# A gated linear attention with a SwiGLU layer behind it: every queue's order written out as a list

## The chip, the cores and the metric

The kernel runs on one core of a Trainium2 chip. The metric is the device time of one execution in microseconds; of the kernel before there are three runs. The core has five instruction queues that run at their own pace and wait for each other by semaphores: PE (TensorE, matmuls), DVE (VectorE), ACT (ScalarE), POOL (GpSimd) and SP (SyncE, which here only issues DMAs). Each queue works strictly in its order, so an instruction that waits holds all that stand behind it.

## The reference

For 4 sequences, 8 heads, 768 steps and a head size of 48, a state is rotated and shrunk by a complex gate at each step:

```python
mag = np.sqrt(a_re * a_re + a_im * a_im)
scale = np.minimum(mag, 0.999) / (mag + 1e-06)
for t in range(S):
    S_re, S_im = ar * S_re - ai * S_im + kv, ar * S_im + ai * S_re
    y[:, :, t] = np.einsum('bhd,bhde->bhe', q[:, :, t], S_re)
```

Here ar and ai are the scaled gate of the step, and kv is the outer product of k and v. The result, 3072 tokens by 384, is normalised by its root mean square and multiplied by a gain (rms_g), and goes through `silu(x @ w_gate) * (x @ w_val) @ w_out` with 1536 hidden columns. All of it is fp32. The weights reach the kernel as pairs of 32-bit words.

## The kernel before, in words

The sequence is cut into 24 chunks of 128 steps, numbered from 0. For each chunk, or each pair from chunk 2 on, `gates` (a generator) turns the gate into phase and magnitude. ACT makes squares, inverse roots, an arc tangent and sines; DVE makes running products and sums (scans), and multiplies q and k by cosine and sine into the tiles `rot` and `kin`. Six DMAs on SP then move these rows into `kq`; the text calls them the moves. A load of gate tables on ACT (`ACT_TABLE_LOAD`) stands wherever the function wanted is not in the tables that are active.

`attend` does one chunk. PE makes the scores of `kq` in small 32-row matmuls, DVE copies them under a causal mask into `am`, and PE multiplies by v (`ve`) and by the carried state. Another set of matmuls (`vn`, `kt`) and two DVE steps with the chunk's `decay` make the next state. For the norm, ACT squares, PE sums over features with a column of ones, DVE writes the mean to `ssv`, POOL raises it to the power -0.5 (`rs`), and for chunks 4 to 21 two DMAs on POOL spread that column to a row in every partition (`sq`, then `row`). DVE multiplies the chunk by `row` and so writes `xT`. For other chunks a matmul with the identity spreads it.

`feed`, `joint` and `down` do the feed-forward layer for two chunks, or for four at the end. `feed` multiplies directly for the first two pairs; `joint` does the later ones with fewer products and sums of weights and inputs on DVE and ACT; `down` is the down projection, whose results leave through `mid` and the two tiles `ot`, each sent by a DMA. The four banks that `feed`, `joint` and `down` share in PSUM are free again when the DVE additions into `ot` have read them. `narrow` makes fp32 weights out of the pairs of words, piece by piece: POOL issues the load, ACT one pass, DVE three passes, into `wg`, `wv` and `wo`. `look` loads the words again later, to test whether the narrowing was exact.

None of these functions issues anything. They call `add`, which notes an operation with its engine, its calls, an estimated duration, and the operations that it depends on (`box` and `note` find these from the slices read and written). When all 2976 are there, the planner (`Flow.schedule`) plays the engines through with these estimates, due times, margins for transfers and a table of shifts by stage (`flow.shift`), and at each step gives the engine the operation that is due first. `issue` then emits the operations in that order; every instruction carries the line of its loop, L751 before. `flow.warm` names one matmul as a filler. The planner puts fillers in front of a PE operation where it expects PE to be idle up to 62 us; they read `rot`, so they begin when the first `rot` row set is written.

A second path, `general`, for inputs that the fast one can't take, stands behind a flag that the fast path writes last (`bad`); it is not run here.

Of the kernel before, what the change touches and what calls it, by code (L numbers as in the profile page):

```python
# [18 lines left out]
P = 128  # L19
# [480 lines left out]

class Flow:
# [14 lines left out]
    MARGIN = {"load": 2.0, "kq": 2.0, "look": 2.0, "raw": 1.5, "attend": 1.5, "rot": 0.6, "decay": 0.6, "norm": 0.3}  # L516
    turn = 0.3
# [3 lines left out]
    TABLES = {"silu": ("S",), "sin": ("S", "N"), "arctan": ("T",), "rsqrt": ("A",)}  # L521

    def __init__(self, nc, rooms):
        self.nc = nc
        self.rooms = rooms
        self.ops = []
        self.seen = {}
        self.stage = None
        self.shift = {}
        self.warm = None  # L530
        self.fillers = []
# [19 lines left out]
    def box(self, ap):  # L551
        t = ap.tensor
        if t.name not in self.rooms:
            return None
        name, row = self.rooms[t.name]
        size = mybir.dt.size(ap.dtype)
        start = ap.offset * size
        p0, lo = divmod(start, row)
        np_, hi = 1, lo + size
        for step, n in ap.ap:  # L560
            if step * size > row:
                p0, np_ = p0 * n, n
            elif step * size == row:
                np_ += (n - 1) * (step * size // row)
            else:
                hi += (n - 1) * step * size
        return name, p0, p0 + np_, lo, hi

    def note(self, op, ap, write):
# [3 lines left out]
        name, p0, p1, lo, hi = b  # L573
        if name.startswith("bank"):
            p0, p1, lo, hi = 0, P, 0, 2048
        kept = []
        for x in self.seen.get(name, ()):
            o, w, q0, q1, l, h = x
            over = q0 < p1 and p0 < q1 and l < hi and lo < h
            if over and (write or w) and o != op["i"] and (not op["group"] or self.ops[o]["group"] != op["group"]):  # L580
                op["deps"].add(o)
            if op["group"] or not (write and p0 <= q0 and q1 <= p1 and lo <= l and h <= hi):
                kept.append(x)
        kept.append((op["i"], write, p0, p1, lo, hi))
# [19 lines left out]
    def dates(self):  # L604
        users = [[] for _ in self.ops]
        self.next = [[] for _ in self.ops]
        for op in self.ops:
            op["behind"] -= op["deps"]
            for d in op["deps"]:
                users[d].append(op["i"])  # L610
            for d in op["behind"]:
                self.next[d].append(op["i"])
        for op in reversed(self.ops):
            due = op["base"] if op["base"] is not None else 1e6
            for u in users[op["i"]]:
                x = self.ops[u]
                stretch = 1.0 if x["eng"] == "PE" else 1.35
                due = min(due, x["due"] - x["dur"] * stretch - (x["land"] or 0.0) - 0.2)
            op["due"] = due
        for op in self.ops:  # L620
            op["due"] += self.shift.get(op["stage"], 0.0)
            if op["late"] is not None:
                op["due"] = max(op["due"], op["late"])
        return users

    def schedule(self):
        users = self.dates()
        left = [len(op["deps"]) + len(op["behind"]) for op in self.ops]
        ready = [0.0] * len(self.ops)
        free = {eng: self.BEGIN.get(eng, 0.0) for eng in self.ENGINES}  # L630
        waiting = {eng: [] for eng in self.ENGINES}
        table = None
        mode = last = None
        for op in self.ops:
            if not left[op["i"]]:
                waiting[op["eng"]].append(op)
        queue = []
        sent = []
        recent = []
        served = held = quiet = 0.0  # L640
        order = 0

        def release(o, end, users=users):
            for u in users[o["i"]]:
                x = self.ops[u]
                margin = o["margin"] if users is not self.next and x["land"] is None and end > self.FROM else 0.0
                ready[u] = max(ready[u], end + self.delay(o, x) + margin)
                left[u] -= 1
                if not left[u]:
                    waiting[x["eng"]].append(x)  # L650

        def able(o):
            return max(ready[o["i"]], quiet) if o["grip"] else ready[o["i"]]

        while True:
            best = None
            for eng in self.ENGINES:
                ops = waiting[eng]
                if ops:
                    if eng == "POOL":  # L660
                        t = min(max(free[eng], ready[o["i"]], held + 0.01 if o["shy"] else 0.0) for o in ops)
                    else:
                        t = max(free[eng], min(able(o) for o in ops))
                    if eng == "SP" and len(sent) >= self.LANES:
                        if "landed" not in sent[-self.LANES]:
                            continue
                        t = max(t, sent[-self.LANES]["landed"])
                    if best is None or t < best[0]:
                        best = (t, eng)
            if queue:  # L670
                o = min(queue, key=lambda o: o["arrives"])
                t = max(served, o["arrives"])
                if best is None or t <= best[0]:
                    queue.remove(o)
                    served = t + o["load"] + 0.05
                    o["landed"] = served + o["slow"] + self.LAND
                    release(o, o["landed"])
                    continue
            if best is None:
                break  # L680
            t, eng = best
            pick = None
            for o in waiting[eng]:
                if able(o) > t + 1e-9 or o["shy"] and t < held:
                    continue
                key = o["due"]
                if o["table"] and table not in self.TABLES[o["table"]]:
                    key += self.switch if t > self.FROM else 4.0
                if eng == "PE" and o["mode"] != mode and t > self.FROM:
                    key += self.turn  # L690
                if pick is None or key < pick[0]:
                    pick = (key, o)
            o = pick[1]
            if eng in self.patient:
                if any(t < able(x) < t + o["dur"] - 0.2 and x["due"] < o["due"] - 50.0 and able(x) < t + 1.5 for x in waiting[eng]):
                    free[eng] = max(free[eng], min(able(x) for x in waiting[eng] if t < able(x)))
                    continue
            waiting[eng].remove(o)
            dur = o["dur"]
            if o["table"] and table not in self.TABLES[o["table"]]:  # L700
                table = self.TABLES[o["table"]][-1]
# [1075 lines left out]
```

## Time and profile before

| what | us |
|---|---|
| median of 3 runs | 693.02 (692.71 to 696.26) |
| profiled execution | 695.43 |
| its span | 693.7 |
| PE busy | 647.2 |
| DVE busy | 561.8 |
| ACT busy | 511.2 |
| ACT table loads | 91.1 (71 of them) |
| mean granted TensorE clock | 0.983 |

In the page's rows a name like `bank<-wo,hT` means that the tile `bank` is written out of `wo` and `hT`, without the tiles' numbers. The time after a group's bar is what its engine was idle just before, and `<-` names what ended most of it. Each fp32 matmul of the program leaves two records. The wait of a queue that only issues (SPq, POOLq) costs nothing by itself; it matters when what it issues later is wanted. The granted clock is a share of TensorE's full rate.

### The profile page before, as it was taken

The page shows a single profiled execution, that of the slowest core. Times are in us where ns is not written, and L with a number is a line of the kernel's source. Part 1 is how long each engine was busy: PE and PEld are TensorE (multiplying, and loading weights), DVE is VectorE, ACT ScalarE, POOL GpSimd, SP SyncE. Part 2 cuts the span into 40 slices and gives each one's busy share as a digit, 9 for nine tenths or more (in the row PEclk, how much of TensorE's full clock was granted, in tenths as well). Part 3 has the DMA queues.
Part 4 walks back from the last instruction along what each step waited for, and adds up shares of the span by engine and source line. Part 5 has one row for each costly group of instructions (what it writes and reads, how often), then busy time and mean ns, then how long its engine had stood idle before and what let it go on. Part 6 is the DMA issues. An engine that isn't in the chain of part 4 may idle for free.

```text
span 693.7 us, 19005 instructions
## 1 busy us (share of the span) xinstructions
PE 647.2 (93%) x7893; PEld 606.5 (87%) x7893; DVE 561.8 (81%) x1050; ACT 511.2 (74%) x854; POOL 65.0 (9%) x108
## 2 busy tenths in 40 slices
PE   0599999999999999999999799999999998999996
PEld 0589876886899999999999799999999998999995
DVE  8989989789999899799889588889898958257362
ACT  8668565986684887786787588678798576797780
POOL 3223030010100000000001000100000000000000
PEclk9969999999999999999999899999999999999999
DMA  9897483455231543543532433443333637733410
GB/s 294 268 260 180 117 253 110 110 126 128 42 74 45 115 135 66 124 97 80 113 71 47 97 94 59 110 86 76 93 68 64 150 113 149 255 130 113 139 47 29
DMA packets 104015, 82.02 MB, mean 118 GB/s; under 512 B 41936, under 2 KB 94416, under 8 KB 103920
## 3 DMA queue, kind: packets, MB, share of 16 engines
q1 hardware_dynamic: 98560, 64.78, 35.5%
q0 software_dynamic: 4416, 15.35, 9.9%
q8 instruction: 64, 1.05, 0.6%
q10 hardware_dynamic: 944, 0.59, 0.3%
q14 instruction: 31, 0.25, 0.1%
HBM read 55.84 MB, written 4.72 MB: 87 GB/s over the span
## 4 chain that ended last, share of the span: by engine, by line
PE 50%; issue 17%; DVE 10%; ACT 10%; DMA 9%; POOL 1%; SPq 1%; ACTq 0%; POOLq 0%; DVEq 0%
PE bank L751 50%; DVE hT L751 3%; DMA sq<-rs 2%; ACT L751 2%; ACT t L751 1%; ACT hT L751 1%; DMA kq<-rot 1%; DVE turns L751 1%; SPq L751 1%; DMA in<-in_a_im_dram 1%; DMA row<-sq 1%; ACT in L751 1%; POOL rs L751 1%; ACT bank L751 1%; ACT turns L751 1%
## 5 line engine op out<-in xcount | busy, mean ns | idle before, releaser
L751 PE MATMUL bank<-wo,hT 128*128 128x192 f32 (+1 forms) x696 | 144.1, 351 | 0.9 <-DVE hT L751 0.8
L751 PEld LDWEIGHTS bank<-wo,hT 128*128 128x128 f32 x696 | 114.8, 190 | 12.9 <-DVE hT L751 1.7
L751 ACT ACT_TABLE_LOAD x71 | 91.1, 1283 | 4.6 <-issue 2.2
L751 PE MATMUL bank<-xT,wg 128*128 128x128 f32 (+1 forms) x488 | 84.2, 305 | 0.7 <-DVE mid L751 0.6
L751 PE MATMUL bank<-xT,wv 128*128 128x128 f32 (+1 forms) x488 | 82.4, 301 | 0.9 <-issue 0.9
L751 ACT ACTIVATE hT<-bank 128x512 f32<-128x512 f32 x100 | 57.8, 594 | 25.7 <-PE bank L751 22.1
L751 PEld LDWEIGHTS bank<-xT,wg 128*128 128x128 f32 x488 | 70.6, 191 | 5.6 <-DVE mid L751 0.8
L751 PEld LDWEIGHTS bank<-xT,wv 128*128 128x128 f32 x488 | 70.1, 191 | 4.2 <-issue 1.0
L751 POOL TENSOR_TENSOR rs<-ssv,mhalf 128x1 f32<-128x1 f32 x24 | 19.0, 790 | 453.1 <-DVE ssv L751 424.8
L751 DVE TENSOR_TENSOR hT<-hT 128x768 f32<-128x768 f32 (+1 forms) x60 | 51.7, 862 | 0.4
L751 PE MATMUL bank<-yg,wg 128*128 128x128 f32 x320 | 50.2, 279 | 0.4 <-ACT hT L751 0.4
L751 ACT ACTIVATE bank<-bank 128x512 f32<-128x512 f32 x60 | 34.9, 583 | 20.7 <-PE bank L751 16.5
L751 PE MATMUL bank<-yg,wv 128*128 128x128 f32 x320 | 48.8, 275 | 0.0
L751 ACT ACTIVATE sg<-bank 128x256 f32<-128x256 f32 (+1 forms) x72 | 38.1, 533 | 13.5 <-PE bank L751 3.8
L751 PE MATMUL bank<-sums,hT 128*128 128x192 f32 x240 | 45.3, 328 | 0.0
L751 PEld LDWEIGHTS bank<-yg,wg 128*128 128x128 f32 x320 | 42.2, 191 | 1.0 <-ACT hT L751 0.5
L751 DVE TENSOR_TENSOR hT<-bank,hT 128x512 f32<-128x512 f32 x50 | 34.3, 687 | 9.9 <-ACT bank L751 4.3
L751 PEld LDWEIGHTS bank<-yg,wv 128*128 128x128 f32 x320 | 42.2, 192 | 0.0
L751 ACT ACTIVATE turns<-in 128x768 f32<-128x768 f32 (+1 forms) x39 | 30.3, 790 | 15.7 <-DVE in L751 11.0
L751 PEld LDWEIGHTS bank<-kq 96*32 96x32 f32 x1536 | 31.3, 114 | 11.9 <-issue 8.4
L751 DVE COPY_PREDICATED am<-causal,bank 128x512 f32<-128x512 int32 x48 | 32.9, 728 | 8.4 <-PE bank L751 8.1
L751 PE MATMUL bank<-am,ve 128*32 128x128 f32 x768 | 38.5, 286 | 1.0 <-DVE xT L751 1.0
(216 smaller groups left out, 1446.6 us busy)
## 6 DMA issues: line engine op xcount, KB each, us to landing
kq<-rot SPq DMA_DIRECT2D x84, 128.0 KB, 2.5
kq<-kin SPq DMA_DIRECT2D x60, 128.0 KB, 2.4
kin<-in_q_dram SPq DMA_DIRECT2D x24, 192.0 KB, 3.0
kin<-in_k_dram SPq DMA_DIRECT2D x24, 192.0 KB, 4.1
out_dram<-ot SPq DMA_DIRECT2D x23, 192.0 KB, 2.3
in<-in_a_re_dram SPq DMA_DIRECT2D x11, 384.0 KB, 5.1
in<-in_a_im_dram SPq DMA_DIRECT2D x11, 384.0 KB, 4.1
vn<-in_v_dram SPq DMA_DIRECT2D x20, 192.0 KB, 3.3
```

What stands on the lines that cost most here:

```text
L751: fn(*args, **kw)
```

## The change

`dates` and `schedule` go, and with them the shifts and what the planner made of margins. In their place stand `ORDER`, a list of all 2977 operations by number, which is the issue order of all five queues at once, and `FILLERS`, how many fillers stand ahead of which operation. `issue` walks the list and asserts that an operation's dependencies are already out.

```diff
+ORDER = [int(i) for i in """
+25 38 2 37 6 3 17 7 0 35 34 24 11 18 4 10 1 41 26 21 20 16 42 15 27 5 206 19 22 204 29 28 63 40 64 36 130 48
...
+""".split()]
+FILLERS = {105: 15, 213: 59, 128: 4, 208: 4, 215: 14, 212: 1, 223: 3, 236: 1, 241: 1}
...
     def issue(self):
-        steps = [(op["order"], op["calls"]) for op in self.ops]
-        steps += [(at, self.warm["call"] * n) for at, n in self.fillers]
-        for _, calls in sorted(steps, key=lambda x: x[0]):
-            for fn, args, kw in calls:
+        done = set()
+        assert sorted(ORDER) == list(range(len(self.ops)))
+        for i in ORDER:
+            assert done >= self.ops[i]["deps"]
+            done.add(i)
+            for fn, args, kw in self.warm * FILLERS.get(i, 0) + self.ops[i]["calls"]:
                 fn(*args, **kw)
...
         flow.stage = "turn", u
-        act(im, im, AF.Arctan, after=roots[-2:])
+        after = roots[-2:]
+        if u == 0:
+            after = [act(warm, warm, AF.Sin, after=after)]
+        act(im, im, AF.Arctan, after=after)
...
-    filler = rots[0][:, 0]
-    flow.warm = dict(after=started, until=WARM, call=[
-        (nc.tensor.matmul, (banks[3][:, 0:C],), dict(lhsT=filler[:, 0:C], rhs=filler[:, C:2 * C], start=True, stop=True))])
-    flow.shift = {
...
-    }
-    flow.schedule()
+    flow.warm = [
+        (nc.tensor.matmul, (banks[3][:, 0:C],), dict(lhsT=ident, rhs=ident, start=True, stop=True))]
```

Besides, `box` and `note` compare the runs of bytes that a slice holds, where they compared its first and last byte; the constants `MARGIN`, `turn` and `TABLES` get other values and a table `PACE` is added, which no instruction depends on any more.

The instructions stay the same but for these: 102 fillers on PE instead of 28, of the identity instead of `rot`; one more ACTIVATE of one column (the sine); and 57 table loads on ACT instead of 71. All else is moved. Three places:

DVE in the head, from the rotation of chunk 1 (`rot_106`) to the first mask copy of chunk 0 (`am_115`); `wg<-wo` and the like are narrowing passes, and ISA is the third of a piece. Before:

```order
L751 TENSOR_TENSOR rot_106<-kin,turns 128x768 x2
L751 TENSOR_SCALAR wv<-wo 128x1536
L751 TENSOR_TENSOR ends<-t_103,t_102 128x3
L751 TENSOR_SCALAR wg<-hT 128x1536
L751 TENSOR_TENSOR ot_134<-ends,ot_134 128x24
L751 TENSOR_SCALAR wv<-hT 128x1536
L751 SCALAR_TENSOR_TENSOR wv<-wo,wv 128x1536
L751 COPY_PREDICATED am_115<-causal,bank_69 128x512
```

and in the change:

```order
L760 TENSOR_TENSOR ot_134<-ends,ot_134 128x24
L760 TENSOR_TENSOR rot_106<-kin,turns 128x768
L760 SCALAR_TENSOR_TENSOR wg<-wo,wg 128x1536
L760 TENSOR_SCALAR wg<-hT 128x1536
L760 ISA wv<-wo,wv 128x3072
L760 SCALAR_TENSOR_TENSOR wg<-hT,wg 128x1536
L760 ISA wg<-wo,wg 128x3072
L760 ISA wg<-hT,wg 128x3072
L760 COPY_PREDICATED am_115<-causal,bank_69 128x512
```

Three pieces are now narrowed in full ahead of the first mask copy; before, it was one in full and parts of three others.

DVE at the norm of chunk 14, from the third of its additions into `mid` up to `xT_96`, with the group's `ot`. Before:

```order
L751 TENSOR_TENSOR mid_137<-mid_136,bank_67 128x192
L751 TENSOR_TENSOR hT<-hT 128x768
L751 TENSOR_TENSOR mid_136<-mid_137,bank_65 128x192
L751 TENSOR_TENSOR mid_137<-mid_137,bank_66 128x192
L751 SCALAR_TENSOR_TENSOR turns<-in_98,carry,zeros 128x256 x3
L751 TENSOR_TENSOR ot_134<-bank_65,mid_137 128x384
L751 TENSOR_TENSOR xT_96<-bank_71,row 128x3x128
L751 SCALAR_TENSOR_TENSOR t_101<-t_101,t_103 128x768
L751 SCALAR_TENSOR_TENSOR in_98<-turns 128x768
L751 SCALAR_TENSOR_TENSOR t_102<-t_101,t_102 128x768
L751 TENSOR_TENSOR ot_133<-mid_136,bank_68 128x384
```

and in the change:

```order
L760 SCALAR_TENSOR_TENSOR turns<-in_98,carry,zeros 128x256 x3
L760 SCALAR_TENSOR_TENSOR t_101<-t_101,t_103 128x768
L760 SCALAR_TENSOR_TENSOR in_98<-turns 128x768
L760 TENSOR_TENSOR ot_134<-bank_65,mid_137 128x384
L760 SCALAR_TENSOR_TENSOR t_102<-t_101,t_102 128x768
L760 TENSOR_TENSOR ot_133<-mid_136,bank_68 128x384
L760 TENSOR_TENSOR ve_120<-yg_125,yg_126 128x128
L760 COPY_PREDICATED am_115<-causal,bank_70 128x512
L760 TENSOR_TENSOR state_122<-state_122,decay_111 96x8x48
L760 COPY_PREDICATED am_115<-causal,bank_72 128x512
L760 TENSOR_TENSOR xT_96<-bank_71,row 128x3x128
```

`xT_96`, which waits for `row`, stood between the two `ot` additions and now stands behind both, and behind the mask copies of chunk 15.

SP at the moves of chunk 9 (`kq_107`). Before:

```order
L751 DMA out_dram<-ot_133 128x384
L751 DMA vn_121<-in_v_dram 128x384
L751 DMA ve_118<-in_v_dram 128x4x48
L751 DMA ve_118<-in_v_dram 32x4x48 x4
L751 DMA in_98<-in_a_re_dram 128x3x256
L751 DMA kq_107<-rot_105 16x8x256 x3
L751 DMA kq_107<-kin 16x8x256 x3
```

and in the change:

```order
L760 DMA kq_107<-rot_105 16x8x256
L760 DMA kq_107<-kin 16x8x256
L760 DMA decay_112<-ends 16x8x2
L760 DMA ve_119<-in_v_dram 32x4x48
L760 DMA ve_118<-in_v_dram 32x4x48
L760 DMA kq_107<-kin 16x8x256
L760 DMA ve_118<-in_v_dram 32x4x48
L760 DMA kq_107<-kin 16x8x256
L760 DMA kq_107<-rot_105 16x8x256
L760 DMA decay_112<-ends 16x8x2
L760 DMA kin<-in_q_dram 128x3x128
L760 DMA kq_107<-rot_105 16x8x256
```

Six moves that stood together now have six other transfers among them. Elsewhere on PE, the new list puts 15 fillers at the very start, 59 behind the first decay matmul, the four first-chunk groups of the first feed-forward stage ahead of those that need the second chunk, and the first down projection ahead of chunk 2's scores; at the end, the flag's matmul comes last on PE and its addition last on DVE.

More of the change, by code (lines that the diff above doesn't have):

```diff
@@ L626, in schedule @@
[L626 to L701, printed above, removed]
-                dur += 1.3
-                self.loads = getattr(self, "loads", 0) + 1
-            if o["shy"] and t == held + 0.01:
-                dur += 0.4
-            if o["grip"]:
-                held = t + dur
-            if o["hush"] and t > self.FROM:
-                quiet = t + dur + self.HUSH
-            if eng == "PE":
-                more = self.between(o, last, t - free["PE"], t)
-                dur += more
-                if not more and t > self.FROM:
-                    late = ready[o["i"]] - (free["PE"] - self.LATE)
-                    if late > 0:
-                        dur += min(self.LATE, late)
-                mode, last = o["mode"], o
-            if eng == "PE" and self.warm and t < self.warm["until"] and all("end" in x for x in self.warm["after"]):
-                since = max([free["PE"]] + [x["end"] + 0.06 for x in self.warm["after"] if not recent])
-                n = int((t - since - 0.3) / 0.43)
-                if n > 0:
-                    self.fillers.append((order - 0.5, n))
-                    recent.append((since, since + 0.43 * n))
-            if eng == "PE":
-                busy = 0.0
-                for b, e in recent:
-                    if e > t - 4.0:
-                        busy += min(e, t) - max(b, t - 4.0)
-                if busy < 2.0:
-                    dur += min(dur, 3.0)
-                recent.append((t, t + dur))
-                del recent[:-12]
-            o["start"], o["end"], o["order"] = t, t + dur, order
-            order += 1
-            free[eng] = t + dur - o["over"]
-            release(o, t + dur, self.next)
-            if o["land"] is not None:
-                o["arrives"] = t + o["lead"]
-                queue.append(o)
-                if eng != "POOL":
-                    sent.append(o)
-            else:
-                release(o, t + dur)
-        assert order == len(self.ops)
@@ L888, in dma @@
         op["lead"] = lead or (1.9 if eng == "POOL" else 1.2)
+        kind = flow.stage and flow.stage[0]
+        op["pace"] = flow.PACE.get((kind, int(load > {"norm": 1.0, "attend": 0.3, "load": 1.0}.get(kind, 9.0) or kind == "look" and row > 2048)))
         return op
```

117 lines of the change are left out of this document (37 added, 80 removed), and 130 rows, old and new, of tables (ORDER, filler).

## The prediction

> **What bounds the kernel now.** I read the stretches first, then who kept TensorE waiting, then the places of the longest waits.
>
> ```profile
> span 693.7 us, 19005 instructions
> 0.00:52.80 52.80, 26.37 (x373) 24.14 (x374) 46.35 (x83) 37.34 (x62) 15.02 (x37) 0.87 0.89 276
> 35.40:49.20 13.80, 13.05 (x216) 11.94 (x220) 11.62 (x15) 9.03 (x15) 4.40 (x4) 0.51 0.90 235
> 60.00:387.00 327.00, 320.91 (x3988) 289.84 (x3988) 294.21 (x529) 243.77 (x376) 35.33 (x45) 1.00 0.44 105
> 387.00:401.00 14.00, 10.04 (x117) 9.27 (x116) 6.39 (x11) 6.17 (x10) 0.54 (x1) 0.76 0.39 87
> 401.00:687.50 286.50, 282.64 (x3358) 276.02 (x3357) 207.18 (x420) 216.86 (x401) 12.96 (x23) 1.00 0.41 105
> ```
>
> After the stretch come its length and the busy time of PE, PEld, DVE, ACT and POOL, then the granted clock. From 60 to 687.5 us PE is busy 613.6 of 627.5 us, so PE bounds the program there and only 13.9 us of its idle time can go. Up to 52.8 us it is DVE: 46.35 us busy against 26.37 on PE, which has no feed-forward work yet.
>
> ```profile
> PE bank L751 <- DVE ot L751: 4.0, 1, 4.0
> PE bank L751 <- ACT bank L751: 2.4, 7, 0.7
> PE bank L751 <- DMA decay<-ends: 1.7, 1, 1.7
> PE bank L751 <- DMA kq<-rot: 1.2, 1, 1.2
> ...
> PE bank L751 <- issue: 0.9, 1, 0.9
> PE bank L751 <- DVE hT L751: 0.8, 3, 0.3
> ```
>
> These are PE's waits from 60 to 687 us (total, times, longest), 13.4 us in all; the rows left out hold 2.4 us. One of them is 4.0 us, and it costs more than it shows:
>
> ```profile
> 363.69 1.33 PE L751 MATMUL bank<-kq 96*32 96x128 f32 x64
> 395.09 0.58 PE L751 MATMUL bank<-zeros 128*128 128x512 bf16 x1 [3.96 <-DVE ot L751]
> 395.60 2.36 PE L751 MATMUL bank<-kq 96*32 96x128 f32 x64
> 386.29 0.53 DVE L751 TENSOR_TENSOR ot<-bank,mid 128x384 f32<-128x384 f32 x1
> 391.41 0.56 DVE L751 TENSOR_TENSOR xT<-bank,row 128x384 f32<-128x384 f32 x1 [4.59 <-DMA row<-sq]
> 394.49 0.55 DVE L751 TENSOR_TENSOR ot<-mid,bank 128x384 f32<-128x384 f32 x1
> 378.12 3.10 POOL L751 TENSOR_TENSOR rs<-ssv,mhalf 128x1 f32<-128x1 f32 x1 [33.28 <-DVE ssv L751]
> 387.35 0.54 POOL L751 DMA_DIRECT2D row<-sq  x1 [5.26 <-DMA sq<-rs]
> ```
>
> Chunk 14's norm row came late: POOL's power took 3.10 us, and the first of two DMAs landed 5.56 us after its issue (381.51 to 387.07). DVE stood 4.59 us at `xT`, and the `ot` addition behind it, which frees PE's bank, could not pass. The same 64 matmuls that take 1.33 us then took 2.36. With a granted clock of 0.76 over 14 us, 3.4 us of full clock are missing there (14 x 0.24). Price of the place: 4.0 + 3.4 = 7.4 us.
>
> **The change, part by part.** The sum is made against the profiled execution's 695.43 us (span 693.7 and 1.7 around it); the median shown is 693.02, so 2.4 us come off at the end.
>
> *The gap at 391 us.* In the new order both `ot` additions of that group stand ahead of chunk 14's `xT`, and so do the next chunk's mask copies. Between `ssv` and `xT` lies 9.5 us of DVE work, by the rows' durations, against 6.9 before. The row needs about this:
>
> ```profile
> L751 POOL TENSOR_TENSOR rs<-ssv,mhalf 128x1 f32<-128x1 f32 x24 | 19.0, 790 | 453.1 <-DVE ssv L751 424.8 <-ACT carry L751 12.9 <-ACT mid L751 11.9
> row<-sq POOLq DMA_DIRECT2D x18, 64.0 KB, 4.0
> sq<-rs POOLq DMA_DIRECT2D x18, 0.5 KB, 2.6
> L751 DVE TENSOR_TENSOR xT<-bank,row 128x384 f32<-128x384 f32 x18 | 10.0, 553 | 9.7 <-DMA row<-sq 9.6
> ```
>
> 0.8 + 2.6 + 4.0 and some 0.6 between them make 8.0 us, which 9.5 covers; and if the row took 13.4 us again, PE's banks would be free by then. Value -7.4 us; bounds -7.4 and 0 (the same wait at another chunk).
>
> *The head.* DVE's work sets when the second chunk's `xT` stands (52.84 us now), after which both halves of the first feed-forward matmuls can run.
>
> ```profile
> L751 DVE SCALAR_TENSOR_TENSOR wg<-wo,wg 128x1536 int32<-128x1536 int32 x2 | 3.5, 1748 | 0.0
> L751 DVE CUSTOM_DVE_ANT_0 wg<-wo,wg 128x3072 uint16<-128x3072 uint16 x2 | 3.5, 1747 | 0.0
> L751 DVE TENSOR_SCALAR wg<-wo 128x1536 int32<-128x1536 int32 x2 | 1.9, 952 | 0.0
> 17.76 1.05 DVE L751 TENSOR_TENSOR_SCAN turns<-in,zeros 128x128 f32<-128x128 f32 x3 [0.86 <-ACT in L751]
> 41.31 0.55 DVE L751 TENSOR_TENSOR state<-bank,decay 96x384 f32<-96x384 f32 x1 [1.23 <-PE bank L751]
> 42.74 0.16 DVE L751 TENSOR_SCALAR ssv<-bank 128x1 f32<-128x1 f32 x1 [0.87 <-PE bank L751]
> 20.90 1.28 ACT L751 ACT_TABLE_LOAD   x1
> 52.79 2.84 PE L751 MATMUL bank<-xT,wg 128*128 128x128 f32 x24
> 60.83 2.84 PE L751 MATMUL bank<-xT,wv 128*128 128x128 f32 x24
> ```
>
> A weight piece is narrowed by three passes, 0.95 + 1.75 + 1.75 = 4.45 us. Ahead of the second `xT` stand five pieces now done in full, where before there were three and a first pass: 22.3 - 14.3 = 8.0 us more. Out of that stretch go one pass of 0.95 and four scans of 0.35 of the third and fourth chunks, 2.3 us. So `xT` moves back 5.7 us, less the idle time that DVE loses. PE gets two things back. The first chunk's four feed-forward groups, half of the four rows from 52.79 to 60.83 (10.7 us, so 5.4), no longer stand behind the second chunk's norm; and one state group of 0.9 us is done earlier. Were DVE as idle as now, PE would stand where it does today: 52.8 + 5.7 + 0.5 + 5.4 - 0.9 = 63.5 us, which is when those groups end now. The gain is thus what DVE's idle time shrinks. It is idle 6.45 us of the first 52.80; the rows show 0.86 behind the first arc tangent and 1.23 + 0.87 behind PE. The sine on a constant loads a table that the arc tangent and the sine share here, so the load at 20.90 goes and the one ahead of the arc tangent moves past some 2 us of other ACT work. PE's answers, at 41 and 42 us, get narrowing work in front of them. I take 2.5 us of the 3.0. Bounds -5.5 (all but the first microsecond) and +1.2 (DVE as idle as now, and one more wait as long as the longest of these, for a weight load that is now wanted sooner).
>
> *Fillers.* 74 more, of which 59 stand in one row ahead of the first chunk's transposes.
>
> ```profile
> 25.32 6.79 PE L751 MATMUL bank<-rot 128*128 128x128 f32 x44 [2.47 <-DVE rot L751]
> 25.29 3.81 SPq L751 DMA_DIRECT2D kq<-rot  x6
> kq<-rot SPq DMA_DIRECT2D x84, 128.0 KB, 2.5
> ```
>
> Each record pair is one filler: 22 took 6.79 us, 0.31 each, so 59 take up to 18.2 us. They begin when the first decay matmul is through, whose input stands after 11.3 us of DVE work where it stood after 17.6 (at 21.5 us), so at 15.2 us, and end by 33.4 us. The first chunk's rows landed by 25.29 + 5 x 0.64 + 2.5 = 31.0 us; they leave DVE after 17.3 us of work instead of 20.4, with two more issues among the moves, so I expect 31.0 - 3.1 + 1.3 = 29.2. What hides them is the narrowing: the first mask copy, which the scores feed, comes after 35.7 us of DVE work where it came after 31.5. Cost 0; without that cover up to 33.4 - 29.2 = 4.2 us.
>
> *ACT.*
>
> ```profile
> L751 ACT ACT_TABLE_LOAD x71 | 91.1, 1283 | 4.6 <-issue 2.2 <-DVE kin L751 1.0
> ```
>
> The main path has 57 loads, 14 fewer: 14 x 1.283 = 18.0 us of ACT's 511. ACT is no bound, so this counts through PE's waits for it, 2.4 us, and the 0.8 for `hT` that ACT feeds.
>
> *The other waits and the moves.* PE's waits after 60 us without the 4.0 are 9.4 us. Two of them, for `kq<-rot` and issue at 84 and 91 us, go, since the first down projection now stands ahead of the third chunk: 2.1. Of the rest I take a third, 2.4. Against that stands SP. Six moves bring a chunk's `kq`; 11 other issues stood among them over the whole program, and now 62. One issue is 3.81 / 6 = 0.64 us, and SP is parked often:
>
> ```profile
> SPq L751 <- PE bank L751: 115.3, 28, 18.9
> ```
>
> The 51 added make the last move of a chunk later by 51 x 0.64 / 24 = 1.4 us on average. One wait of 1.2 us in 24 chunks is today's whole cost, so most of it is covered; I take +2.0. Net -2.5; bounds -9.4 and +20 (below). The tail stays: the flag's addition moves behind the last `ot`, under the last output's 2.7 us landing. The numbers of the planner that changed act on nothing that is issued, since the written list alone sets the order: 0.
>
> Sum: -7.4 - 2.5 - 0 - 2.5 = -12.4, so 695.43 - 12.4 = 683.0, and on the footing of the median 693.02 - 12.4 = 680.6. I forecast 681 us.
>
> **The rivals.**
>
> *Full clock through the first chunks.*
>
> ```profile
> 26.00:28.00 2.00, 2.00 (x11) 1.00 0.52 140
> 30.00:32.00 2.00, 2.00 (x19) 1.00 0.62 133
> ```
>
> From 35.40 to 49.20 us PE was busy 13.05 of 13.80 us at a clock of 0.51. If the fillers keep it at 1.0, half of that busy time, 6.4 us, goes, were all of it on the path: 681 - 6.4 = 675. For it: 2 us held 11 records of fillers at first and 19 four microseconds later, so fillers do lift the rate (the clock column has no record of the start). Against it: PE was busy all through the half clock, so being busy did not lift it, and DVE leads there. The Trainium skill (TensorE: Matmul & The Clock Gate, "What's actually happening") says that the array goes to full rate after one busy window of about 3.4 us and falls back after an idle one. By that rule this rival would hold; the trace agrees for the start of the fillers and for the gap at 391 us, and disagrees from 35 to 49 us.
>
> *The order does not do what it says.* The late row comes at another chunk. The cover between `ssv` and `xT`, summed from durations, is 5.7 us at chunk 20 and 6.6 at chunk 13, below 8.0. One wait of 7.4 us there and the moves' +2.0 doubled: 681 + 7.4 + 2.0 = 690. With no gain in the head 692.5: no change. For it: POOL's power once took 3.10 us. Against it: most of today's 18 waits at `xT` sum to 9.6 us and stop PE in just two places.
>
> *Slower: SP parked among the moves.* The mechanism is a load for a later chunk that waits for its buffer and stands between two moves of `kq`; SP holds the rest, PE reaches the scores, in its order, and stops. SP waits 115.3 us for PE today, 18.9 at the longest, so a parked issue is no rarity; but in 20 of 24 chunks nothing stands among the moves today, and in the new order in 6 of 24. A wait of 4 us costs 7.4 with its half clock. Two such make 681 + 14.8 = 696, three 703. It decides from the second. The Trainium skill (DMA: Bandwidth & Descriptors, "Anatomy of one DMA — SWDGE (gpsimd) path") says that the wait is on the issuing sequencer and not in the DMA engines, which speaks against such interleaving; SP's rows above agree.
>
> **How the numbers follow.** Forecast 681 (676 to 687): 0.55. Full clock and a shorter head, 675 (668 to 676): 0.20. No net change, 692: 0.13. SP parked, 699: 0.12. A measurement tells 0.5%, 3.5 us, from no change. Faster holds the first two and a little of the third: 0.78; same 0.10; slower 0.12. Range 670 to 697: the rival of 675 whole, no change whole and the first half of the slower one.
>
> **What would show it.** Right: no PE wait on `ot` near 391 us and no half clock after 60 us; the four feed-forward groups end at about 61 us; 57 table loads; PE's waits from 60 us to the end near 7 us. The head is wrong if the second `xT` stands after 58 us. The moves are wrong if PE's waits for `kq` or `decay` exceed 3.2 us. The whole is wrong if a new PE wait above 3 us appears, with a clock of about 0.5 behind it.

## The result, and the profile after

| kernel | median, us | runs | lowest to highest |
|---|---|---|---|
| before | 695.22 | 20 | 691.64 to 703.31 |
| changed | 690.0 | 20 | 684.7 to 695.75 |

The ratio of changed to before is 0.993 (95% interval 0.9905 to 0.9956): 5 us faster, where I had forecast 12.4. The ratios leave out runs more than 1.5% above the fastest of their kernel, here one of the changed kernel's 20, so they need not be the quotient of the medians. The profiled execution of the changed kernel took 684.7 us, the lowest of its 20, while the profiled execution of before (695.43) stands at its median. So the two profiles differ by 10.7 us and the medians by 5.2; half of the question is what the first profile of the changed kernel does not show.

The stretches and some of PE's waits from 55 to 680 us (5.4 us in all) of the changed kernel, in the columns of the prediction:

```profile
span 682.9 us, 19269 instructions
35.40:49.20 13.80, 11.61 (x260) 10.37 (x248) 13.01 (x15) 8.94 (x13) 4.05 (x7) 1.00 1.09 304
60.00:387.00 327.00, 322.51 (x4076) 293.48 (x4076) 295.28 (x538) 236.62 (x375) 28.09 (x47) 1.00 0.46 107
387.00:401.00 14.00, 13.95 (x215) 13.73 (x215) 13.08 (x24) 11.23 (x21) 0.00 (x0) 1.00 0.45 123
```

```profile
PE bank L760 <- DVE xT L760: 1.8, 2, 1.5
PE bank L760 <- ACT bank L760: 0.9, 4, 0.3
...
PE bank L760 <- DMA kq<-rot: 0.5, 1, 0.5
```

At 387 to 401 us PE is now busy 13.95 us at full clock, against 10.04 at 0.76. The wait for `ot` is gone, and in this profile there is no half clock from 60 us to 675 us. The row of chunk 14 was not even late. The timeline of the changed kernel at that place, DVE first and then POOL (start, length, instruction, and in brackets the idle time before it and what ended it):

```profile
377.79 0.16 DVE L760 TENSOR_SCALAR ssv<-bank 128x1 f32<-128x1 f32 x1 [0.68 <-PE bank L760]
377.86 0.34 DVE L760 TENSOR_TENSOR mid<-mid,bank 128x192 f32<-128x192 f32 x1
...
385.98 0.55 DVE L760 TENSOR_TENSOR ot<-mid,bank 128x384 f32<-128x384 f32 x1
...
388.35 0.54 DVE L760 TENSOR_TENSOR xT<-bank,row 128x384 f32<-128x384 f32 x1
...
378.03 0.56 POOL L760 TENSOR_TENSOR rs<-ssv,mhalf 128x1 f32<-128x1 f32 x1 [26.44 <-DVE ssv L760]
...
381.99 0.53 POOL L760 DMA_DIRECT2D row<-sq  x1 [2.52 <-DMA sq<-rs]
```

The head went the other way. The second `xT` was to stand by 58 us and stands at 60.1; the feed-forward groups of the first two chunks were to end at about 61 us and end at 67.2, where they ended at 63.7 before. The timeline of PE, DVE and SP there:

```profile
50.48 0.30 PE L760 MATMUL bank<-am,ve 128*32 128x128 f32 x2 [2.34 <-issue]
...
56.55 0.16 DVE L760 TENSOR_SCALAR ssv<-bank 128x1 f32<-128x1 f32 x1 [2.77 <-PE bank L760]
...
59.56 0.56 DVE L760 TENSOR_TENSOR xT<-yg,bank 128x384 f32<-128x384 f32 x1 [0.55 <-PE bank L760]
...
36.77 0.57 SPq L760 DMA_DIRECT2D in<-in_a_re_dram  x1
37.39 17.43 SPq L760 DMA_DIRECT2D ve<-in_v_dram  x6
```

PE stops between two matmuls of `am` with `ve`, the values of chunk 1. Four pieces of them now stand on SP behind the two gate loads of the next pair. In the view of transfers (count, KB of each, median us from issue to landing) the last two of the four, issued about 39 us, read:

```profile
ve<-in_v_dram SPq DMA_DIRECT2D x2, 24.0 KB, 10.2
```

The profile puts PE's 2.34 us down to "issue", so it names no one; the run that moves the pieces (below) bears out that they were the cause.

### The profile page after: what moved, and what is told of

The parts are those of the page before. It is cut to its first block, busy times and chain, and to the rows that moved or that the text cites. A ratio compares the mean times of both kernels' runs of the same rounds, so it can differ in the third digit from the quotient of the medians.

```text
span 682.9 us, 19269 instructions
## 1 busy us (share of the span) xinstructions
PE 656.0 (96%) x8039; PEld 618.2 (91%) x8041; DVE 558.8 (82%) x1050; ACT 493.4 (72%) x841; POOL 61.6 (9%) x108
## 4 chain that ended last, share of the span: by engine, by line
issue 54%; PE 22%; DMA 9%; DVE 7%; POOL 3%; SPq 2%; ACT 1%; POOLq 0%; DVEq 0%
PE bank L760 22%; DMA sq<-rs 7%; SPq L760 2%; POOL rs L760 2%; DVE wg L760 1%; POOL row L760 1%; DVE wo L760 1%; DVE turns L760 1%; DMA in<-in_a_re_dram 1%; DVE t L760 1%; DMA row<-sq 1%; DVE rot L760 1%; DMA ve<-in_v_dram 1%; DVE wv L760 1%; DVE hT L760 1%
## 5 line engine op out<-in xcount | busy, mean ns | idle before, releaser
L760 PE MATMUL bank<-wo,hT 128*128 128x192 f32 (+1 forms) x696 | 141.5, 350 | 0.0
L760 ACT ACT_TABLE_LOAD x57 | 73.1, 1283 | 3.3 <-issue 2.2
L760 POOL TENSOR_TENSOR rs<-ssv,mhalf 128x1 f32<-128x1 f32 x24 | 15.0, 626 | 436.3 <-DVE ssv L760 388.7
L760 PEld LDWEIGHTS bank<-sums,hT 128*128 128x128 f32 x240 | 39.1, 190 | 1.0 <-issue 0.4
L760 ACT ACTIVATE t<-t 128x768 f32<-128x768 f32 (+1 forms) x39 | 30.7, 789 | 11.7 <-DVE t L760 11.4
L760 DVE TENSOR_TENSOR bank<-bank,hT 128x512 f32<-128x512 f32 x30 | 20.9, 696 | 20.0 <-ACT hT L760 16.4
```

The source lines that it names most:

```text
L760: fn(*args, **kw)
```

## The experiments

Each median is given beside that of the kernel before, measured side by side with it, and ratios stand with their 95% intervals. Kernels that were not measured side by side are compared by their ratios, and the text says so.

**What the place, the rest and the head are worth.**

*The changed kernel again.* No edit.

> The changed kernel once more, for a second profile and a second interval. Its profiled execution took 684.7 us, the lowest of 20 whose median is 690.0, so 5.3 us of a usual execution are not in that profile. Theory A, waits that come and go: a usual execution shows one or two more stops of PE after 60 us, each with a stretch of half clock behind it, as the 3.96 us stop of the kernel before was with 3.4 us; PE's waits from 55 to 680 us then sum to 8 to 12 us instead of 5.4. Theory B, one clock or one speed that differs as a whole: the waits stay near 5.4 us and the 5 us are spread over the span. Ratio to before for both: 0.993, 0.990 to 0.996.

689.84 against 695.66, 0.9914 (0.989 to 0.9938). Its profiled execution took 692.87 us, and it differs from the first one from the head on. Its timeline of POOL and PE, and its transfers from 22 to 37 us:

```profile
23.28 0.20 POOL L760 COPY junk<-hT 1x1 int32<-1x1 int32 x1 [2.54 <-DMA hT<-in_w_gate_dram]
23.75 0.86 POOL L760 DMA_DIRECT2D hT<-in_w_val_dram  x1 [0.26 <-issue]
...
36.57 0.87 PE L760 MATMUL bank<-ident,kq 96*128 96x96 f32 x4 [5.19 <-DMA kq<-rot]
...
41.85 2.33 PE L760 MATMUL bank<-kq 96*32 96x128 f32 x64
...
109.63 0.66 PE L760 MATMUL bank<-am,ve 128*32 128x128 f32 x8 [1.10 <-ACT turns L760]
```

```profile
kq<-rot SPq DMA_DIRECT2D x12, 128.0 KB, 6.7
hT<-in_w_val_dram POOLq DMA_DIRECT2D x1, 1536.0 KB, 10.7
```

and the moves of the kernel before, from 25 to 36 us:

```profile
kq<-rot SPq DMA_DIRECT2D x12, 128.0 KB, 2.4
```

POOL issues a weight piece just as the moves begin; the 12 moves take a median of 6.7 us where they took 2.4. PE stops 5.19 us and comes back at half rate (the 64 score matmuls take 2.33 us, not 1.33). The prediction had named this as the sign that the whole is wrong: a new wait above 3 us with a clock of about 0.5. Later, near 110 us, a second stop has half clock behind it (the stretch, in the prediction's columns):

```profile
110.00:114.00 4.00, 4.00 (x69) 3.62 (x61) 3.70 (x6) 0.49 (x1) 0.00 (x0) 0.50 0.17 47
```

So theory A holds in part: PE's waits from 55 to 680 us sum to 7.6 us, a little below its 8 to 12, and the stops differ from execution to execution. The longest is before 60 us, but the one near 110 us costs more: against the first profile this execution is 2.7 us behind at the second `xT` (62.8 against 60.1 us) and 6.2 us behind at the fourth (121.7 against 115.6).

*The place at 391 us alone*, in the kernel before:

```diff
+TENSOR_TENSOR xT (chunk 14), behind the second ot and both mask copies
-TENSOR_TENSOR xT (chunk 14), between the two ot
```

> The kernel before with one step moved and nothing else: on DVE the xT of chunk 14 goes behind the second ot addition of that group and the two mask copies behind it, as in the new order. Theory A, the late row at 391 us is there in every execution, as my price of 7.4 us supposed: 688 us, 0.989 of before. Theory B, the row was late by chance in the profiled execution (POOL's power took 3.10 us where the mean is 0.79): the wait is there in few executions, and the time is 0.998 to 1.000 of before. Between the two, 0.994, the wait is there in every second execution.

688.53 against 695.66, 0.9897 (0.9874 to 0.992). The row is late in this execution as well, and nobody waits for it (timeline of POOL and DVE, then the stretch):

```profile
377.71 3.10 POOL L751 TENSOR_TENSOR rs<-ssv,mhalf 128x1 f32<-128x1 f32 x1 [33.46 <-DVE ssv L751]
...
386.64 0.53 POOL L751 DMA_DIRECT2D row<-sq  x1 [4.95 <-DMA sq<-rs]
...
388.97 0.55 DVE L751 TENSOR_TENSOR ot<-mid,bank 128x384 f32<-128x384 f32 x1
...
392.98 0.54 DVE L751 TENSOR_TENSOR xT<-bank,row 128x384 f32<-128x384 f32 x1
```

```profile
387.00:401.00 14.00, 14.00 (x264) 13.43 (x263) 11.92 (x21) 11.73 (x21) 0.18 (x1) 1.00 0.48 106
```

This one moved step is worth 7.1 us, more than the whole change brings. Theory A.

*The old head with the new rest*: the old order and 28 fillers up to the first matmul that needs both halves of the first feed-forward stage, then the new order.

> The old order up to the first matmul that needs both halves of the first feed-forward stage (about 63 us), with the old number of fillers, 28, of the identity; the new order for all the rest. Theory A, the new head costs: at equal work PE stands 2.5 to 3 us behind the kernel before from 47 to 80 us in the two profiles, so this kernel is 2.5 us below the changed one, about 0.989. Theory B, the new head gains in usual executions by its fillers and full clock, as I had forecast: this kernel is 2.5 us above the changed one, about 0.997.

685.32 against 695.66, 0.9847 (0.9821 to 0.9874), and 4.5 us below the changed kernel. The place and the rest together bring 10.3, of which 3.2 are the rest; the new head with its fillers gives 4.5 back. This run exchanges two things, the order of the head and the number of fillers, 28 for 102; the runs on fillers below take them apart. It also has a seam: at 83.1 us PE waits 2.07 us for `hT`, a wait that neither profile of the changed kernel has.

*The counterpart*: new head, old rest.

> The counterpart of the old head with the new rest: the new order with its fillers up to the first matmul that needs both halves of the first feed-forward stage, and the old order for all the rest. Theory A, the new head costs 4.5 us by itself, whatever follows: 4 to 5 us above before, 1.006. Theory B, head and rest hang together (the later narrowing, which the new head has done sooner, is what the new rest needs): the same as before within 1.5 us, or below.

714.54 against 693.92, 1.0285 (1.0248 to 1.0321). Neither theory: the seam makes stops of its own. The longest of PE's waits from 20 to 680 us:

```profile
PE bank L760 <- DMA kq<-rot: 7.7, 2, 4.5
PE bank L760 <- ACT sg L760: 5.9, 1, 5.9
PE bank L760 <- DVE ot L760: 3.9, 1, 3.9
```

It prices the seam, and says nothing about the head alone.

**What the head loses by transfers.** Four repairs, each a step put back to where the old order had it.

*Value pieces.*

```diff
+SP: ve_119 x4, ahead of the first moves
-SP: ve_119 x4, behind the two gate loads in_99
```

> The changed order, but the four value pieces of chunk 1 (the transfers into ve) stand on SP ahead of the first moves instead of behind the two gate loads of the next pair. In the profile of the changed kernel PE stops for 2.34 us at 48 us, between the matmuls of am with ve, and the last of these four pieces landed at 50.39, 11.1 us after its issue; a half clock from 51.5 to 54.9 follows. Theory A, that late transfer makes the head long: the stop goes, and 1.7 us of the half clock with it, so the second xT stands near 56 us instead of 60.1 and the time is 4 us below the changed kernel's of the same call, about 0.987 of before. Theory B, DVE leads the head whatever lands when: the second xT moves by less than 1 us and the time by less than 1 us, 0.992 to 0.994.

687.14 against 695.66, 0.9887 (0.9858 to 0.9917). The stop at 48 us is gone from its profile and the second `xT` stands 3.2 us sooner, at 56.9; the median is 2.7 us below the changed kernel's. Theory A in kind, though the intervals of the two overlap.

*The fourth weight piece.*

```diff
 POOL: touch of the second piece (junk<-wo)
+POOL: hT<-in_w_val_dram
 POOL: touch of the third piece (junk<-hT)
-POOL: hT<-in_w_val_dram
```

> The changed order with one POOL step moved: the issue of the fourth weight piece (hT out of in_w_val) goes back to where the old order had it, straight behind the touch of the second piece, and no longer behind the touch of the third. In the two profiles of the changed kernel that issue came at 28.1 us and at 23.75 us (before: 18.7), and the piece landed at 36.5 and 34.45; in the second case the moves of chunk 0 landed up to 36.9 instead of 31.9 and PE stood 5.19 us. Theory A, this load against the moves is the rest of the head's loss and most of its scatter: of the 4.5 us by which the old head was better 2 to 3 come back, 687 us, 0.988 of before, and the runs lie closer together. Theory B, the loss is the value pieces alone and narrowing work on DVE: no more than 0.5 us.

686.67 against 694.87, 0.9882 (0.9849 to 0.9915). The time is theory A's, though its interval too overlaps the changed kernel's (0.989 to 0.9938); the runs do not lie closer together as it had them (6.3 us from lowest to highest, 3.5 in the six of the changed kernel).

*Both.*

> Both repairs at once: the weight piece's issue as in the old order, and the four value pieces of chunk 1 ahead of the moves. Theory A, these two transfers are what the head lost: the time is that of the old head with the new rest or better (685.3), since the head's feed-forward work that I had forecast to come 2.5 us sooner then does: 683 to 685, 0.982 to 0.985 of before, the second xT at 56 us or less. Theory B, DVE's narrowing ahead of the second xT costs by itself: 687 to 688, 0.988.

685.88 against 694.87, 0.9871 (0.9829 to 0.9914): between the theories. The two gains do not add up: the runs cannot tell both from either one. What two later profiles with both repairs showed was a third race, in the first 16 us; here the timeline of POOL, SP and DVE in the kernel whose moves stand together (below):

```profile
5.70 0.92 POOL L760 DMA_DIRECT2D wo<-in_w_gate_dram  x1
...
6.22 0.59 SPq L760 DMA_DIRECT2D kin<-in_q_dram  x1
...
15.99 0.56 DVE L760 TENSOR_TENSOR kin<-kin,t 128x384 f32<-128x384 f32 x1 [3.94 <-DMA kin<-in_q_dram]
```

*q and k of chunk 0 ahead of its value pieces on SP*, with both repairs and then alone:

```diff
+SP: kin<-in_q_dram, kin<-in_k_dram (chunk 0), ahead of ve_118 x3
-SP: the same, among and behind ve_118 x3
```

> Both repairs and a third: on SP the loads of q and k of chunk 0 go ahead of the chunk's value pieces, as the old order had them. In two profiles of the new order with repairs POOL's first weight piece was issued at 5.7 us, ahead of that load of q (SP reached it at about 6.2 us), DVE then waited 2.6 and 3.9 us for it, and the first rotated rows stood at 23.9 and 25.0 us instead of 21.9; in the other profiles the weight piece was issued at 6.0 to 6.6 and there was no such wait. Theory A, this race is decided anew in each execution and is what is left of the head's loss and scatter: no execution waits for q, and the time is 2 us below both repairs' 685.9, so 683 to 684, 0.983 of before, with runs that lie closer together. Theory B, the time lost there is hidden behind the narrowing and its cover: 685 to 687.

> The changed order with the third repair alone: q and k of chunk 0 ahead of its value pieces on SP. Theory A, the race against the first weight piece is lost in a part of the executions of the changed kernel and costs 3 us each time: 688 to 689, 0.990 of before. Theory B, in the changed kernel the late weight piece and the late value pieces hide it: 690, 0.993.

With all three repairs 682.8 against 693.92, 0.9833 (0.9797 to 0.987); alone 687.35, 0.9915 (0.9885 to 0.9946). Alone it cannot be told from the changed kernel; the three together can. What the third adds to the other two is not shown: the intervals of two and three overlap, and with three the runs lie no closer together (679.38 to 687.21). The profiled execution with three was the longest of its six (687.21 us) and shows a fourth late transfer, in the timeline of ACT and PE:

```profile
46.63 0.84 ACT L760 ACTIVATE t<-in 128x768 f32<-128x768 f32 x1 [4.01 <-DMA in<-in_a_re_dram]
...
49.94 0.66 PE L760 MATMUL bank<-am,ve 128*32 128x128 f32 x8 [3.51 <-ACT yg L760]
```

The granted clock was at half from 49.3 to 56.1 us there.

*The third yg copy of chunk 0 ahead of that step on ACT.*

```diff
+ACT: yg (chunk 0, third), ahead of t<-in_99
-ACT: yg (chunk 0, third), behind turns<-in_99
```

> The three repairs, and on ACT the third yg copy of chunk 0 goes ahead of the two steps that wait for the next pair's gate loads, as the old order had it. In the profile with three repairs (687.2 us, the longest of its runs) the second gate load landed at 46.6 us beside a weight piece that POOL had issued at 34.4, ACT stood 4.01 us at the first of these steps, and PE waited 3.51 us for yg, with half clock from 50 to 54 us; in the profile of the changed kernel ACT stood 1.0 us there. Theory A, that is a fourth transfer which is late in some executions: no execution loses it, the median falls by 1 to 2 us from the 682.8 of three repairs, 681 to 682, and the longest of the runs stays below 686. Theory B, it happened in that one execution: the same as three repairs within 1 us.

683.8 against 694.63, 0.9869 (0.9821 to 0.9917), the longest run 691.14. No gain over three repairs: theory B, or an effect below the 3 us that these runs can tell.

**The moves.**

```diff
-SP: 62 other issues among the six moves of a chunk
+SP: the same 62, each behind the last of the six
```

> Both repairs, and the six moves of each chunk stand together on SP: the 62 other issues that stood among them go behind the last of the six. Theory A, as I predicted, the split moves cost 2.0 us by PE's waits for kq: the time is 2 us below that of both repairs alone. Theory B, nearly all of it is covered (PE waited 0.5 us for kq in the first profile of the changed kernel, not at all in the second): within 1 us. Theory C, what stood among the moves was wanted there, and holding it back delays loads: 2 us or more above.

684.57 against the 685.88 of both repairs, with the same 694.87 of before; the ratios are 0.9883 (0.984 to 0.9926) and 0.9871. Theory B.

**The fillers.** In the first of these kernels some of the 28 fillers stand where their bank holds a result of the program, which they overwrite; the instructions and their order are otherwise the same, and it stands for its time only. The others have 20 fillers ahead of the first transposes and 8 behind.

```diff
-FILLERS = {105: 15, 213: 59, 128: 4, 208: 4, 215: 14, 212: 1, 223: 3, 236: 1, 241: 1}
+FILLERS = {128: 22, 239: 2, 250: 2, 253: 1, 255: 1}                        the first (two repairs)
+FILLERS = {213: 20, 128: 4, 208: 4}                                        the others
```

> Both repairs, and 28 fillers at five places instead of 102 at nine. What I predicted, fillers cost nothing and give nothing: the time of the kernel with both repairs, within 1 us. Theory B, fillers keep the clock at full rate through the first chunks: the clock from 35 to 49 us is near 0.5 again as in the kernel before, and the time is 3 to 6 us above that of both repairs. Theory C, the long row of fillers holds the first scores (it ended at 31.5 us in the two profiles, where the rows of chunk 0 can land near 28): the time is 1 to 3 us below.

> All three repairs and 28 fillers instead of 102: 20 ahead of the first transposes and 8 in the two places behind, none at the start and none among the later matmuls. Theory A, as predicted, fillers neither cost nor give: within 1 us of the three repairs. Theory B, they hold the clock: half clock between 35 and 60 us, 2 to 3 us more. Theory C, the long row holds PE: 1 to 3 us less.

> The same four repairs with 28 fillers instead of 102. Theory A, fillers are free: as with 102 fillers, within 1 us. Theory B, the long row of fillers in front of the first transposes costs, as 680.3 against 682.8 with three repairs hints: 2 to 3 us less than with 102, so 679, 0.978 of before.

> The changed kernel with nothing else than its fillers cut from 102 to 28, 20 of them ahead of the first transposes. My prediction gave the 74 more a cost of 0, hidden by the narrowing, and up to 4.2 us without that cover. Theory A, 0: 690, 0.993 of before, within 1 us of the changed kernel. Theory B, they are a part of what the head lost, by 2 to 4 us: 686 to 688, 0.988 to 0.990.

| | with 102 | with 28 |
|---|---|---|
| changed kernel | 690.0 and 689.84; 0.993, 0.9914 | 683.83; 0.984 (0.9808 to 0.9873) |
| two repairs | 685.88; 0.9871 | 684.8; 0.9849 (0.9812 to 0.9886) |
| three repairs | 682.8; 0.9833 | 680.32; 0.980 (0.9769 to 0.9831) |
| four repairs | 683.8; 0.9869 | 680.89; 0.9796 (0.9765 to 0.9827) |

(The two cells of the changed kernel were not measured side by side, so compare their ratios; those of each other row were.) Fewer is less time each time, by 1 to 6 us. With repairs the intervals overlap; for the changed kernel itself the interval with 28 lies below both of those with 102. So fillers are not free.

This also corrects the reading of the two heads. With 28 fillers and no repair the new head stands at 0.984, the old head with 28 and its seam at 0.9847: at equal fillers the two cannot be told apart. The 4.5 us by which they differed are covered by the fillers alone. By the ratios the three repairs are worth 6 us with 102 fillers (0.9833 against 0.9914 to 0.993) and 3 us with 28 (0.980 against 0.984, intervals overlapping). So the two losses overlap: either remedy alone brings back most of what both bring.

Which fillers cost?

```diff
+FILLERS = {213: 59, 128: 4, 208: 4}                                        the long row kept
+FILLERS = {105: 15, 213: 20, 128: 4, 208: 4, 215: 14, 212: 1, ... }        the long row cut
```

> The changed kernel with only its long row of fillers (59 ahead of the first transposes, and the 8 behind it); the 15 at the start and the 20 among the later matmuls go. Cutting all 102 to 28 took 6 us off the changed kernel, where I had costed them at 0. Theory A, the long row is what costs, as it runs to 31.4 us where rows can land before: the time stays near the changed kernel's, 688 to 690, 0.992. Theory B, the others cost (at the start, or among the matmuls of the first two chunks, where each one stands in PE's way): 684 to 685, 0.985.

> The counterpart: the long row is cut from 59 to 20 and all other fillers of the change stay, 63 in all. Theory A, the long row costs: 684 to 685, 0.985. Theory B, the others cost: 688 to 690, 0.992. If both this and its counterpart stand near 687, the cost goes by the number of fillers.

684.9, 0.9854 (0.9814 to 0.9893), with the long row kept; 687.5 against the same 695.38, 0.9889 (0.9852 to 0.9925), with it cut. Both lie between the changed kernel and the one with 28, nearer to theory B of each: the 35 others seem to cost more than the long row. The intervals overlap too much to show it, and the second also overlaps the changed kernel's.

*None at all*, with four repairs:

> The four repairs and no filler at all. Theory A, fillers give nothing at all: as with 28, 680.9, 0.980 of before, or 1 us less. Theory B, the 28 still buy clock for the first scores (in the profile with 28 the clock was 0.73 from 20 to 35 us and 0.68 from 35 to 49): 2 us or more above 680.9.

681.89 against 695.38, 0.981 (0.9777 to 0.9843): the same as with 28 (0.9796, not measured side by side), so fillers bought nothing here. PE's timeline of that kernel:

```profile
31.23 0.87 PE L760 MATMUL bank<-ident,kq 96*128 96x96 f32 x4 [15.43 <-DMA kq<-rot]
...
32.85 2.36 PE L760 MATMUL bank<-kq 96*32 96x128 f32 x64
39.67 0.90 PE L760 MATMUL bank<-ident,kq 96*128 96x96 f32 x4 [4.46 <-DVE am L760]
...
45.02 2.36 PE L760 MATMUL bank<-kq 96*32 96x128 f32 x64
```

The scores run at half rate (2.36 us), and then PE waits 4.46 us for DVE's mask copy anyway.

The three repairs, and the four, with 28 fillers are the best of all: 0.980 of the kernel before, and 8 to 9 us below the changed one by the ratios.

How the fillers cost is not shown; the profiles give only a weak hint where. Between 103 and 116 us the granted clock was 0.74 in the second profile of the changed kernel and 0.87 in those with three repairs, with the long row kept and with it cut: four of the eleven profiles of this order (with and without repairs) that have 63 to 102 fillers, and none of the five that have 28 or none. From the second to the fourth `xT` the changed kernel took 59.0 us in its second profile and 55.0 with 28 fillers. That stop comes 50 us and more after the last filler, and no run was made to find what ties the two.

## Why the prediction was wrong, point by point

*The gap at 391 us, -7.4:* right. The step alone brings 7.1 us. The bound of 0, the same wait at another chunk, did not come: PE's two waits for `xT` sum to 1.8 us.

*The head, -2.5, bounds -5.5 and +1.2:* wrong. With its 102 fillers it came out 4.5 above the old head, and at equal fillers level with it (0.984 and 0.9847, not measured side by side), so the 2.5 was not there. I counted what DVE, PE and ACT have to do and priced a transfer that comes late by "one more wait as long as the longest of these", 1.2 us, and "for a weight load". What came late were the small transfers beside the weight loads: values and rotated rows in the two profiles of the changed kernel, where they stopped PE for 2.34 and 5.19 us with half clock on top, and q in two profiles with repairs, where DVE stood 2.60 and 3.94 us. I had compared the order of DVE and PE in the head row by row, and that of SP and POOL only for the moves. With three of these transfers back in their old places and 28 fillers, the same head is some 3 us better than the old one (0.980 and 0.9847, not measured side by side, and the intervals touch). That is about the 2.5 that I had taken, but it is not shown clear of noise.

*Fillers, 0, up to 4.2 without cover:* wrong, and the larger of the two steps that failed: cutting 102 to 28 and nothing else took 5 to 6 us off the changed kernel. The cover that I named held in the first profile, where the long row of fillers ended at 31.5 us and the first mask copy came at 39.22 without a wait (PE, then DVE):

```profile
15.83 15.65 PE L760 MATMUL bank<-ident 128*128 128x128 f32 x118
...
39.22 1.33 DVE L760 COPY_PREDICATED am<-causal,bank 128x512 f32<-128x512 int32 x2
```

So the cost came by another way than the one that I had priced. Which one stays open: in the profile with 28 the head is no shorter (the second `xT` ends at 62.0 us, with 102 at 60.1).

*ACT, 57 loads:* right in number (57, 73.1 us in all). What that alone is worth no run shows.

*The other waits and the moves, -2.5:* near in sum, as the rest of the order is worth 3.2 (with whatever the seam costs in that run), but partly by luck, since two errors offset each other. The +2.0 for the split moves was too much: from 55 us on PE waited 0.5 us for `kq`, and putting the moves together changed nothing that can be measured. So the waits brought some 3 us where I had taken 4.5.

*The planner's numbers, 0:* nothing speaks against it.

The sum with the measured terms is -7.1 - 3.2 + 4.5 = -5.8, against -5.2 by the 20 runs. It is no check, since the three terms are the steps between four medians measured side by side; it shows that the missing 7 us lie in the head with its fillers, +4.5 where I had -2.5. With the head's transfers and the fillers put right the order gives 680.3 and 680.9 us, near the forecast 681, in part by luck: it is then 13.6 and 13.7 us below the kernel before, and the forecast was 12.4 below a median of three runs that lay 2.2 us under that of 20.

*The rivals.* Full clock through the first chunks came true as a clock in the first profile (1.00 from 35 to 49 us, before 0.51; 0.69 in the second) and brought nothing that can be measured. The reason given against it, that DVE leads there, fits the kernel without fillers, where PE at half rate still waited for the mask copy. That the order does not do what it says, 692, came nearest in time for another cause; no late row moved to another chunk. SP parked among the moves did not happen. None of them put the loss into the head's transfers or the fillers.

## What to carry to other kernels

When an order is rewritten, compare the issue order of every queue that starts transfers, not only the engines that compute: here 24 KB loads that moved back in SP's order landed after 10 us and stopped PE for 2.34. A profile shows one execution; where the profiled one is the lowest of its runs, take a second profile before believing the gain. Fillers that keep TensorE's clock up have to be priced by leaving them out: here none did as well as 28, and 102 did worse. And when one part of a kernel is exchanged for another, see that nothing else goes with it; here the fillers went with the head.

## What the runs showed of the hardware

*0.2 us decide a race.* POOL's touch of the third weight piece began at 23.28 us in the second profile of the changed kernel and took 0.20 us. POOL's and DVE's timeline in the first profile:

```profile
23.49 4.68 POOL L760 COPY junk<-hT 1x1 int32<-1x1 int32 x1 [4.32 <-DMA hT<-in_w_gate_dram]
...
23.34 0.93 DVE L760 TENSOR_SCALAR wv<-wo 128x1536 int32<-128x1536 int32 x1
24.19 0.54 DVE L760 SCALAR_TENSOR_TENSOR in<-turns 128x384 f32<-128x384 int32 x1
24.65 1.74 DVE L760 SCALAR_TENSOR_TENSOR wv<-wo,wv 128x1536 int32<-128x1536 int32 x1
```

DVE's passes had just begun, and the touch of one element ended only at 28.17 us; the weight piece behind it was issued at 28.1 us instead of 23.75. The same is seen at chunk 14: in the old order POOL's power of 3.10 us starts 0.17 us after DVE has begun this group,

```profile
377.95 1.99 DVE L751 TENSOR_TENSOR_SCAN t<-t,t 128x128 f32<-128x128 f32 x6
379.86 0.93 DVE L751 SCALAR_TENSOR_TENSOR in<-turns 128x768 f32<-128x768 f32 x1
380.93 0.35 DVE L751 TENSOR_TENSOR mid<-mid,bank 128x192 f32<-128x192 f32 x1
```

and ends at 381.22, when DVE has turned to an addition that reads a bank. In the new order such an addition stands right behind `ssv`, and the power takes 0.56. The power is about half of the lateness. The other half is the first DMA behind it: issued at 381.51 beside the moves and a gate load on SP, it landed after 5.6 us, and in the new order, where the moves had been issued by 376.4 and this DMA at 378.89, after 2.8. Both profiles with the old order at this place show both delays, so the late row seems to come from the order itself. The Trainium skill (SBUF — State Buffer, "Who interferes with whom") says that a DVE instruction with two inputs in SBUF contends with a GpSimd instruction that reads SBUF, that the port pair they share is an exclusive lock, and that the order of issue decides who blocks. These rows agree; that the touch stayed blocked over five DVE instructions in a row is more than the page states. No run took the DVE work away to prove it.

*Large and small transfers share.* The median of the moves was 2.4 us before and 6.7 beside a weight piece of 1.5 MB that another queue had issued. The Trainium skill (DMA: Bandwidth & Descriptors, "Issuing engines are not separate DMA queues") says that transfers of all issuing engines run on the same 16 DMA engines and interleave; the two medians agree.

*A clock column without a record reads 1.00.* The first clock record in the profile of the kernel without fillers stands at 52.6 us. Its stretches show

```profile
35.40:49.20 13.80, 9.53 (x172) 8.72 (x176) 12.19 (x14) 6.71 (x12) 2.48 (x5) 1.00 0.90 296
```

and yet its 64 score matmuls took 2.36 us, at 32.85 and again at 45.02 us, as they do at half clock. The duration of a known group tells the rate where the column cannot.
